# Loads of V on one queue, w_in further up, and a new order for the first quarter of an attention and MLP kernel

## The chip, the cores and the metric

The kernel runs on one core of one Trainium2 chip. The metric is the device time of one execution in microseconds (us). Time before is the median of three runs; one more execution was recorded by the profiler.

## The reference

```python
# q, k, v: (8, 8, 576, 64), batch, heads, tokens, head size; float32
q_d, k_d, v_d = means over groups of 4 tokens          # 144 pooled tokens
out_up    = repeat(softmax(scale * q_d @ k_d.T) @ v_d, 4 times along the tokens)
out_local = softmax(scale * q @ k.T where |i - j| < 4) @ v
attn = out_up + out_local
x = attn.transpose(0, 2, 1, 3).reshape(4608, 512)      # 8 batches x 576 tokens
h = x @ w_in                                           # 512 x 2048
g = h - tanh(h)
out = g @ w_out                                        # 2048 x 512, float32
```

So it is a coarse attention over pooled tokens plus a narrow band attention, for every head, followed by an MLP over the tokens of all batches.

## The kernel before

**Work and its units.** Heads are worked in 32 pairs; pair p belongs to batch p // 4. One pair goes through these steps, with their lines in before (the changed code is one line longer from line 409 on, so that there the same steps read one higher). SyncE loads q, k into staging tiles `st` (L389, for later pairs into `Tw` and other tiles that are free at that time) and V in two halves, one per head, into `vst` (`load_v`, L415). Casts to bf16 give `qr` (L550) and `vw` (L476). TensorE transposes q, k (L557 and L580 for what is left over), copies take them to `kt`, `kq` (L562, L567, L612, L617). TensorE sums groups of four tokens (L664, L667), and a cast puts them into `qkd` (L672); for later pairs sums `half` (L638, L649, L653) and L643 do it on POOL or DVE. Scores: L701 and L711 (band), L717 (pooled). ScalarE (ACT) takes the exps into `E` (L722, L726, L730), the band mask is multiplied in at L757, on DVE or POOL. V is pooled by L507 and copied to `vp` (L511). The 18 matmuls of L771 give the outputs with their sums; r = 1/sum (L787), `ln` = output times r (L789), both on DVE. TensorE transposes back (L814), `od` (L818 on ACT, L820 on DVE) holds the pooled part, and two joins (L807) write the pair's rows of `xT`. From pair 8 on, DMA transposes issued by SyncE take the place of some of the TensorE ones.

**MLP.** One block is 512 tokens of a batch (64 are left over per batch and done apart, L996, L1114 and others). h = L848, 64 matmuls of 128 x 512 for a block that is done plainly (block 0 and 1 are); tanh on ACT (L860); the subtraction into `gT` on DVE (L863). `mm2` for block 0 is L1142, 64 matmuls; later blocks use L1284, with sums `Tw` of parts of w_out that DVE makes once (L1193). w_in comes in four tiles of 512 KB, issued by GpSimd (POOL, `load_w`, L457), and w_out likewise (L461). Block 1's L848 needs all four `xT` parts of pairs 4 to 7.

**What sets the order.** The program records every operation with its reads and writes in a `Plan`; `emit` then issues them in the order of the table `TURNS` (two digits in base 62 per operation). `ENGINES` has one letter per operation that may run on more than one engine (A, D, P for ACT, DVE, POOL), in the order in which they are recorded. `BANKS` seats results in PSUM. `FILL` puts warm-up matmuls ahead of an operation, and `BEHIND` lists pairs of operations of which the second waits for the first, between DVE and POOL. Each engine works through its own instructions in that order, and an instruction that issues a DMA waits in the order of its engine like any other.

Of the kernel before, what the change touches and what calls it, by code (L numbers as in the profile page):

```python
# [101 lines left out]
def kernel(  # L102
# [51 lines left out]
    TURNS = (
        "000I0J0G0H0307060E0F0K0L04050Q0R010O0P0W0X0e0f0C0M0N0S0T100Y0Z110g0h020a0b1215130D0A160U"
        "0V171H1P18141I0B1J191L1Q1A1K1R221M1N0m0n0i0j1O242R231T1j1k1B251S1C1f1d1g1e1u1U0c0d1W1v1w"
        "2S1y0k0l1x2Z091V2I2J0y2T082G2H1z1D2V291E2W0o0p261F2U1X1l1m212X27201n1o2z1Y2b1Z0z391p1q2a"
        "0q0r2d282c2n2o1r1G2e311h1i1s2f2p2q2g2A2K2L322Y1t3A3B2B2O2y5H2C3C3D302D2P3G5I332E1a353E0s"
        "0t2M2N5J34362v2h2F373N3O5K5L5P2i1b5e5f383F0u0v5M5S2w5N2r2s2j5O5Q3H5U5R3I3J5v662Q2k683K5B"
        "5T1c635E5V3L3d2l5C5x2m643j3k5y3M3l3e5D5F3f3g5X3p3q5W0w0x3m3h3v3r3n3w3i3P3Q5w3s5Y3t2t2u3o"  # L160
        "413x615k5l3y3u5z3z4243604744404D4E4548623T3U495Z654A464F4G4B4J6b5a674H4P3V3W4Q6B4R2x4K4L"
        "4I696c4S5g5h4M6e4C4N3X3Y3R3S5s5b6g6A4V4W4b4O6d4c5c4d4T4X5d4Y6U4h5t4U4i4Z5m5n4j4e4k6T4a6C"
        "4l4n6V6D4o6E4f4t4u4p6W4v4g6X6Z6f6F6Y7A6j4z4q6G5G4w4m504r513Z3a526H6a5556534s577B6Q4x5854"
        "7f7C6R7g4y6h3b3c7D597E72887F6i8d8e5A5u7I6k7G71896l7l6m74758E8F7H8j736n6y76778k6z966o7J6K"
        "6L977K6I6J9C7L5i5j7m8K6p5q5r7M6w6x8L7N7r7O5o5p8p78CF6M6N9D79CC7s6u6v7x9f8Q6q6r7y9g6s6t8R"
        "9Z9I9a8S8q9T9b9cCG7z9h9i7X9jCE6O6P7Y7b9k7P7Q7Z9J9l9v9w7c6SCB8v9t9u7d8w9U7V7WCD9O8x9P7R7S"
        "7eAA9m9W7h9V9X9Y7i7a7n9QCH7o7j9nAB7p7k7t70ACAD809d9o9p849eAGAd7uA1A27qAe9q9zA0AH7vA79r81"
        "7T7U9sA8BD857w82ELEMAIAh9x9y86838AAgAJ8B878GAiAjCI8H8C8MAEAM8VAFATAU8I8NAVAW8DAm8WAKAbAc"
        "Ao8J8O8ZB0B18XAL8aBGBH8fAq8PAn8gAN8Y8bBFB2B38l8h8cA9ApAk8m8iBEAt8rAOBMBIBJ8sAP8n8yAr8z8o"
        "8tDt92BcBdBN908u93AXAYBAAl91DyIgIh989EBaBbAs9FBBENEO94CJBOBPBgBh99BQ9K95Dx9AAuBiDzE09G9L"  # L170
        "9BBqEaBKBrBLE39HA5A6CLCMEJEKAv9MBsAwE4B8B9BtBRBkBlByBTEb9NE5A3A4BjE6E7BzEcEdBSCREACSCKAQ"
        "8T8UE8C0E1C1CYARBUC6CZCoE2C7C8CpBVF8BWCuC9CAEgCvEHEIASAxD0EiIcIdAyBXEhEkD2AZAaBYDuD3BZB6"
        "B7AfF7EjAzD8EPEQElEVD9ERESEeDvBmEfIeIfBuE9BvF9FAEmDEBnEBBwFDB4B5DGEnBxDHFfEwExBoDMEXEYEC"
        "IFDNEDCXEWEuEvC2F2C3ETEUDSCaFEC4BpCbBCCgIGC5F3ChFVFWFeFFCmFGFgEEEFCNFICnCTFHCUFTFUDTFBFJ"
# [232 lines left out]
    def load_v(p):  # L407
        b, j, s = p // NP, p % NP, seat_v(p)
        for i in range(2):
            base = v[b, 2 * j + i]  # L410

            aside = (p, i) in ASIDE

            def issue(i=i, base=base, aside=aside):
                (nc.scalar if aside else nc.sync).dma_start(out=vst[s][:, i], in_=bass.AP(  # L415
                    tensor=base.tensor, offset=base.offset,
                    ap=[[D, 128], [STEP * D, NT], [1, D]]))
# [1138 lines left out]
```

## Time and profile before

| what | value |
|---|---|
| median of three runs | 309.12 us (308.51 to 309.83) |
| profiled execution | 309.13 us |
| its span | 307.4 us |
| mean granted TensorE clock | 0.992 |

The span is the time from the first to the last recorded instruction; about 1.7 us of the execution lie outside. PE is TensorE's matmuls, PEld its weight loads, DVE is VectorE, ACT ScalarE, POOL GpSimd, SP SyncE; a name with q behind it (ACTq) is that engine's instruction queue, where DMA issues and waits stand. A releaser, given as `<-`, is what ended an engine's idle time.

### The profile page before, as it was taken

How to read it: one execution, taken by the hardware profiler on the slowest of the kernel's cores; microseconds unless marked ns; L12 is line 12 of the kernel's file. 1: busy time of each engine (PE TensorE's matmuls, PEld its weight loads, DVE VectorE, ACT ScalarE, POOL GpSimd, SP SyncE). 2: the span in 40 equal slices, each digit the busy share in tenths (PEclk: the TensorE clock that was granted, in tenths of full speed). 3: DMA queues.
4: the chain of work that ended last, by engine and by line, in shares of the span. 5: the costliest groups of instructions: out<-in, count | busy, mean ns of one | idle time of the engine just before them, and what ended most of it. 6: DMA issues, size and time to landing. Idle time of an engine off the chain costs nothing.

```text
span 307.4 us, 8109 instructions
## 1 busy us (share of the span) xinstructions
PE 296.4 (96%) x3091; PEld 210.9 (69%) x3100; DVE 266.6 (87%) x493; ACT 224.1 (73%) x403; POOL 157.2 (51%) x213
## 2 busy tenths in 40 slices
PE   8598999999999999999999999999999999999994
PEld 3476555545577755875577755555988888889983
DVE  2578888679998988999998889999999999998783
ACT  2588786279888786988958988898877898875300
POOL 5247756026864466337873278456524364626550
PEclk9979999999999999999999999999999999999999
DMA  7999999999999999999899999979989426000333
GB/s 220 271 264 249 246 228 152 210 235 220 218 241 281 242 216 234 291 175 273 210 262 220 284 222 173 278 193 260 188 227 218 146 28 189 1 3 2 136 122 87
DMA packets 121191, 60.83 MB, mean 198 GB/s; under 512 B 88896, under 2 KB 119104, under 8 KB 121152
## 3 DMA queue, kind: packets, MB, share of 16 engines
q1 hardware_dynamic: 114656, 54.94, 76.5%
q0 software_dynamic: 4224, 4.19, 8.3%
q10 hardware_dynamic: 2272, 1.18, 1.6%
q8 instruction: 24, 0.39, 0.5%
q14 instruction: 15, 0.12, 0.1%
HBM read 44.04 MB, written 9.44 MB: 174 GB/s over the span
## 4 chain that ended last, share of the span: by engine, by line
PE 88%; DVE 5%; DMA 4%; issue 1%; ACT 1%; ACTq 0%; SPq 0%; DVEq 0%
PE ps L1284 27%; PE ps L848 26%; PE ps L958 8%; PE ps L771 6%; PE ps L996 5%; PE ps L1142 4%; PE ps L701 3%; PE ps L1114 2%; PE ps L1081 2%; DMA st<-in_q_dram 2%; DMA sr<-in_q_dram 2%; PE ps L814 1%; DVE E L757 1%; PE ps L717 1%; PE ps L507 1%
## 5 line engine op out<-in xcount | busy, mean ns | idle before, releaser
L848 PE MATMUL ps<-xT,w_in_sb 128*128 128x512 bf16 x384 | 91.5, 379 | 0.0
L1284 PEld LDWEIGHTS <-gT 128*128 128x128 bf16 x672 | 64.5, 98 | 12.3
L863 DVE TENSOR_TENSOR gT<-ps,u 128x512 bf16<-128x512 f32 x96 | 64.2, 684 | 6.8 <-ACT u L860 5.6
L860 ACT ACTIVATE u<-ps 128x512 f32<-128x512 f32 x96 | 56.4, 599 | 16.3 <-PE ps L848 14.5
L848 PEld LDWEIGHTS <-w_in_sb 128*128 128x128 bf16 x384 | 35.4, 98 | 35.6
L550 POOL CAST qr<-st 128x512 bf16<-128x512 f32 x42 | 25.4, 613 | 41.3 <-DVE Tw L1193 15.5
L1284 PE MATMUL ps<-w_out_sb,gT 128*128 128x256 bf16 x336 | 43.4, 273 | 0.0
L1284 PE MATMUL ps<-Tw,gT 128*128 128x256 bf16 x336 | 42.5, 273 | 0.0
L722 ACT ACTIVATE E<-ps 128x912 bf16<-128x912 f32 x32 | 29.9, 934 | 7.1 <-PE ps L711 5.8
L789 DVE TENSOR_TENSOR ln<-ps,r 128x768 bf16<-128x768 f32 x32 | 30.6, 955 | 0.8
L628 ACT COPY kt<-kq 128x576 bf16<-128x576 bf16 x23 | 27.3, 1185 | 1.4 <-DMA kq<-qr 1.1
L757 DVE TENSOR_TENSOR E<-E,mask 128x1152 bf16<-128x1152 bf16 x31 | 23.5, 760 | 3.8 <-ACT E L726 3.5
L771 PEld LDWEIGHTS <-E 128*128 128x128 bf16 x576 | 21.9, 98 | 6.0 <-DVE E L757 1.4
L638 POOL TENSOR_TENSOR half<-kq 128x576 f32<-128x576 bf16 x16 | 20.5, 1279 | 8.4 <-ACT u L860 3.5
L730 ACT ACTIVATE E<-ps 128x576 bf16<-128x576 f32 x32 | 21.0, 657 | 1.4 <-PE ps L717 1.4
L771 PE MATMUL ps<-vw,E 128*128 128x65 bf16 x320 | 19.2, 195 | 1.3 <-DVE E L757 1.0
L643 POOL TENSOR_TENSOR qkd<-half 128x288 bf16<-128x288 f32 x21 | 16.7, 797 | 5.8 <-DVE r L787 2.0
L1219 DVE TENSOR_TENSOR gT<-gT 128x2048 bf16<-128x2048 bf16 x14 | 17.2, 1231 | 0.2
L1370 POOL TENSOR_TENSOR y<-y,keep 128x512 f32<-128x512 f32 x8 | 10.2, 1278 | 13.4 <-DVE E L757 4.8
L996 PE MATMUL ps<-xT,w_in_sb 128*128 128x128 bf16 x256 | 16.8, 219 | 0.0
L1306 ACT COPY y<-ps 128x512 f32<-128x512 f32 x19 | 11.0, 587 | 7.5 <-PE ps L1284 6.7
L771 PE MATMUL ps<-vpr,E 128*128 128x65 bf16 x128 | 16.5, 195 | 0.0
(183 smaller groups left out, 596.4 us busy)
## 6 DMA issues: line engine op xcount, KB each, us to landing
vst<-in_v_dram SPq DMA_DIRECT2D x54, 160.0 KB, 4.2
st<-in_q_dram SPq DMA_DIRECT2D x28, 256.0 KB, 3.7
st<-in_k_dram SPq DMA_DIRECT2D x28, 256.0 KB, 5.0
out_dram<-y SPq DMA_DIRECT2D x14, 512.0 KB, 4.3
v<-in_v_dram SPq DMA_DIRECT2D x20, 256.0 KB, 2.7
w_in_sb<-in_moe_w_in_dram POOLq DMA_DIRECT2D x4, 512.0 KB, 8.4
w_out_sb<-in_moe_w_out_dram POOLq DMA_DIRECT2D x4, 512.0 KB, 6.6
vr<-in_v_dram SPq DMA_DIRECT2D x8, 128.0 KB
```

Of the source, the lines that this page charges most:

```text
L550: (eng, ns, lambda dst=dst, src=src, fn=fn: fn(out=dst, in_=src), port)
L628: ("ACT", 1180, lambda: A.copy(out=ktv, in_=src), False),
L722: A.activation(out=E[s][:, :, E0:E0 + 456], in_=at(s1)[:, :, PS0:512], func=AF.Exp, scale=SCALE)
L757: eng.tensor_tensor(out=el, in0=el, in1=mask.unsqueeze(1).to_broadcast([128, 2, S]), op=ALU.mult)
L771: T.matmul(po[:, hh, 65 * n:65 * n + 65], E[s][:, hh, e:e + 128], vv, start=start, stop=stop)
L789: op("DVE", 960, lambda: V.tensor_tensor(out=ln[s].rearrange("p n (h d) -> p h n d", d=D), in0=blocks()[:, :, :, 0:64], in1=r[s].unsqueeze ...
L848: T.matmul(at(name)[:, 0, :], w_in_sb[:, dc, fc * 128:(fc + 1) * 128], xT[dc][:, c0:c0 + S].rearrange("p (c g) -> p c g", c=4)[:, :, 0:128 ...
L860: op("ACT", 600, lambda: A.activation(out=u[us], in_=at(name)[:, 0, :], func=AF.Tanh), reads=[("hd", kb, fc)], writes=[("u", us)], uses=[n ...
L863: op("DVE", 690, lambda: V.tensor_tensor(out=gT[g][:, fc, :], in0=at(name)[:, 0, :], in1=u[us], op=ALU.subtract), reads=[("hd", kb, fc), ( ...
L958: T.matmul(at(("hz", kb, G, bk))[:, 0, 256 * x:256 * x + 256], left(k, x), right(k), start=(first and x == 0 and k == 0), stop=(k == 1), s ...
L996: T.matmul(at(name)[:, 0, 128 * f:128 * f + 128], w_in_sb[:, dc, (f0 + f) * 128:(f0 + f) * 128 + 128], xT[dc].rearrange("p (b c g) -> p b ...
L1284: T.matmul(dst, left[:, f, 128 * j:128 * j + 128], right[:, f, :], start=(first and e == 0 and f == 0 and (j == 0 or apart)), stop=(e == 1 ...
```

## The change

Three things. First, `ASIDE` is replaced by an empty `WAY`: before, the first halves of V for pairs 2 and 3 were issued by ScalarE, now SyncE issues all of them. Second, the tables: the first 719 of the 2263 entries of `TURNS` are put in another order (this reaches to about 90 us), and the rest is the same entry for entry. The set of operations is the same. Third, `ENGINES` moves 58 operations to another engine, and `BANKS`, one entry of `FILL` (another bank) and `BEHIND` go with the new order. Of `TURNS` a line stands here for all.

```diff
-        "000I0J0G0H0307060E0F0K0L04050Q0R010O0P0W0X0e0f0C0M0N0S0T100Y0Z110g0h02
...
+        "0I0J0G0H0E0F0K0L0Q0R0O0P0W0X0e0f000307060405010M0N0S0T0Y0Z0g0h0a0b0U0V
...
     ENGINES = (
-        "APADDADAADPPDDPPDDADDDDAPPDADDAADDDPDDDDDAADDADAADDDAAADDDPPAPPPAADAPPPDAAPAPADADPPPDDAA"
-        "APADAAPPPDAAPPDDAAPPPDDAAAADDPDADDAADDDDAPPPDDPPDAAAPPAAPPDDAAPPPAAPPDDPPADDADDADAAPPDAP"
+        "DDADDADDDPPDDAPADDADADDADADDADAADAADDDAADADDADAPAAADDAADDPPPDPPAADADPPPDAAAPAAADDPPDDDDA"
+        "PDAADAPDPDAAPPPDAAPDDPDAAADPPPDADPAAPDDDDPPPDDPPDAAAPPDADPDDAAPPPAAPPDDPPADDADDADAAPPDAP"
...
         "ADPDDPPPDDD"
     )
     BANKS = (
-        "0123453012067016731120212706021330112130022310312010302101013121001113020110023303011200"
-        "2131010210231012301102321001203101010110123031002311201210012130120131010102030210302321"
+        "0123721011626324512321305410230320200313520012100322130311102113011012230320101300011230"
+        "1132100233101032011002301001203101010110123031002311201210012130120131010102030210302321"
     )
     FILL = (
-        "15717 2b71 2A71 3B41 2D11 5S31 3H31 6671"
+        "15717 2b71 2A71 3B41 2D11 5S31 3H01 6671"
     )
     BEHIND = (
-        "0211 1H12 1D1V 0z20 1t2f 5I30 5Q5N 635B 5w5W 6562 6c2x 6d6A 5u6i AACD ABCH AmAF AnAL DxC"
-        "J F8CZ FfFD DFFn MUFt GAGb IrJ6 JNK7 MZJs NBKu OELA LqNn ODLO O7OQ QoNy RYOp RZP8 T3Rd S"
-        "WPQ PiSi TVTU TaRk TPUO TnUY TmTO WZU7 WeWc WfVu XWX6 XcXP Z5Yy ZqZ4 ZpZH"
+        "0211 1H12 1B19 2y2f 5v5W 5C6A 6b6c 7A6Z 717C 7273 7H6i 9fCG 9aCH 9TCI AACF AnAF A9AL BEA"
+        "k DxCJ F8CZ FfFD DFFn MUFt GAGb IrJ6 JNK7 MZJs NBKu OELA LqNn ODLO O7OQ QoNy RYOp RZP8 T"
+        "3Rd SWPQ PiSi TVTU TaRk TPUO TnUY TmTO WZU7 WeWc WfVu XWX6 XcXP Z5Yy ZqZ4 ZpZH"
     )
 
     const = ctx.enter_context(tc.tile_pool(name="const", bufs=1))
...
     def seat_qk(p):
         return p if p < 2 * NP else p % NST
 
-    ASIDE = ((2, 0), (3, 0))
+    WAY = {}
 
     def seat_v(p):
         return p if p < 9 else (p - 9) % NVST
...
         for i in range(2):
             base = v[b, 2 * j + i]
 
-            aside = (p, i) in ASIDE
-
-            def issue(i=i, base=base, aside=aside):
-                (nc.scalar if aside else nc.sync).dma_start(out=vst[s][:, i], in_=bass.AP(
-                    tensor=base.tensor, offset=base.offset,
-                    ap=[[D, 128], [STEP * D, NT], [1, D]]))
-            load(680 if aside else 500, issue, [("vst", s, i)], 940, 10 * p - 3000 + 5,
-                 eng="ACT" if aside else "SP")
+            eng = WAY.get((p, i), "SP")
+
+            def issue(i=i, base=base, eng=eng):
+                {"SP": nc.sync, "ACT": A, "POOL": GP}[eng].dma_start(
+                    out=vst[s][:, i], in_=bass.AP(
+                        tensor=base.tensor, offset=base.offset,
+                        ap=[[D, 128], [STEP * D, NT], [1, D]]))
+            load({"SP": 500, "ACT": 680, "POOL": 770}[eng], issue, [("vst", s, i)], 940,
+                 10 * p - 3000 + 5, eng=eng)
 
     def load_v4(p):
         b, h0, s = p // NP, 2 * (p % NP), p % NV4
```

What it does to the order of three engines, at the places that matter below. On ACT, near the program's start, before: `vst3` and `vst2` are the V tiles of pairs 3 and 2, `E0` and `E1` the exps of even and odd pairs, `qkd1` the pooled q and k of pair 1.

```order
L617 COPY kq0_94<-rT0_81 128x4x16
L612 COPY kt1_97<-rT0_81 128x4x16
L415 DMA vst3_86<-in_v_dram 128x5x64
L415 DMA vst2_85<-in_v_dram 128x5x64
L672 CAST qkd1_100<-ps_138 128x2x144
L722 ACTIVATE E0_113<-ps_138 128x2x456
L726 ACTIVATE E0_113<-ps_138 128x2x120
L730 ACTIVATE E0_113<-ps_138 128x2x2x144
```

The same place after:

```order
L551 CAST qr1_93<-st1_74 128x2x4x64
L673 CAST qkd0_99<-ps_138 128x2x144
L551 CAST qr0_92<-st2_75 128x2x4x64
L613 COPY kt1_97<-rT0_81 128x4x16
L727 ACTIVATE E0_113<-ps_138 128x2x120
L731 ACTIVATE E0_113<-ps_138 128x2x2x144
L723 ACTIVATE E0_113<-ps_138 128x2x456
L673 CAST qkd1_100<-ps_138 128x2x144
L723 ACTIVATE E1_114<-ps_138 128x2x456
```

The two DMA issues are gone; `qkd` of pair 0, a cast of pair 1 and one of pair 2 stand ahead of the exps, the exps of pair 0 are in another order, and `qkd1` follows them instead of preceding them.

On POOL, where its first casts and loads of weights stand, before (`w_in_sb` is w_in, `vrs` and `vrp` are sums over the left-over tokens of V):

```order
L550 CAST qr1_93<-st1_74 128x2x4x64 x2
L442 TENSOR_TENSOR vrp_107<-vrs_106 128x64
L550 CAST qr0_92<-st2_75 128x2x4x64
L445 TENSOR_TENSOR vpr0_111<-vrp_107,hsel_108 128x520
L476 CAST vw1_89<-vst1_84 128x10x64
L457 DMA w_in_sb_71<-in_moe_w_in_dram 128x4x512
L476 CAST vw3_91<-vst3_86 128x10x64
L550 CAST qr1_93<-Tw1_135 128x2x4x64 x2
L457 DMA w_in_sb_71<-in_moe_w_in_dram 128x4x512
```

And after:

```order
L551 CAST qr1_93<-st1_74 128x2x4x64
L439 TENSOR_TENSOR vrs_106<-vr0_104 128x128
L443 TENSOR_TENSOR vrp_107<-vrs_106 128x64
L458 DMA w_in_sb_71<-in_moe_w_in_dram 128x4x512
L541 CAST rr1_80<-sr1_78 128x2x4x64
L458 DMA w_in_sb_71<-in_moe_w_in_dram 128x4x512 x2
L650 TENSOR_TENSOR half_98<-kt0_96 128x144x2
L551 CAST qr1_93<-Tw1_135 128x2x4x64
```

The first tile of w_in is issued behind one cast and two sums, where before casts of q, k and V for three pairs stood ahead of it; the second and the third are issued together; the casts of `vw` are on other engines at this place.

On DVE, ahead of block 1: the outputs of pairs 6 and 7 (`ln0`, `ln1`), the joins into `xT2`, `xT3` and the sums `Tw`, before:

```order
L757 TENSOR_TENSOR E1_114<-E1_114,mask_66 128x2x576
L550 CAST qr0_92<-st0_73 128x2x4x64
L787 RECIPROCAL r1_116<-ps_138 128x12
L789 TENSOR_TENSOR ln1_118<-ps_138,r1_116 128x2x6x64
L807 TENSOR_TENSOR xT2_69<-ps_138,od0_121 128x3x4x28
L807 TENSOR_TENSOR xT2_69<-ps_138,od0_121 128x2x4x30
L820 COPY od1_122<-ps_138 128x144
L807 TENSOR_TENSOR xT3_70<-ps_138,od1_122 128x3x4x28
L807 TENSOR_TENSOR xT3_70<-ps_138,od1_122 128x2x4x30
L1193 TENSOR_TENSOR Tw2_136<-w_out_sb_72 128x1024
L1193 TENSOR_TENSOR Tw0_134<-w_out_sb_72 128x1024
```

And after:

```order
L790 TENSOR_TENSOR ln0_117<-ps_138,r0_115 128x2x6x64
L1194 TENSOR_TENSOR Tw0_134<-w_out_sb_72 128x1024 x2
L1194 TENSOR_TENSOR Tw2_136<-w_out_sb_72 128x1024
L788 RECIPROCAL r1_116<-ps_138 128x12
L790 TENSOR_TENSOR ln1_118<-ps_138,r1_116 128x2x6x64
L1194 TENSOR_TENSOR Tw1_135<-w_out_sb_72,Tw0_134 128x1024
L821 COPY od1_122<-ps_138 128x144
L808 TENSOR_TENSOR xT3_70<-ps_138,od1_122 128x3x4x28
L808 TENSOR_TENSOR xT3_70<-ps_138,od1_122 128x2x4x30
L644 TENSOR_TENSOR qkd0_99<-half_98 128x2x144
L808 TENSOR_TENSOR xT2_69<-ps_138,od0_121 128x3x4x28
L808 TENSOR_TENSOR xT2_69<-ps_138,od0_121 128x2x4x30
```

Three sums of w_out now stand (two and one) between `ln` of pair 6 and `r` of pair 7 and a fourth ahead of the joins, the joins of pair 6 come last, and the mask of pair 7 (`E1`) is no longer on DVE; POOL has it.

More of the change, by code (lines that the diff above doesn't have):

```diff
@@ L154 @@
     TURNS = (
[L155 to L169, printed above, removed]
@@ L170 @@
-        "8tDt92BcBdBN908u93AXAYBAAl91DyIgIh989EBaBbAs9FBBENEO94CJBOBPBgBh99BQ9K95Dx9AAuBiDzE09G9L"
-        "9BBqEaBKBrBLE39HA5A6CLCMEJEKAv9MBsAwE4B8B9BtBRBkBlByBTEb9NE5A3A4BjE6E7BzEcEdBSCREACSCKAQ"
+        "0I0J0G0H0E0F0K0L0Q0R0O0P0W0X0e0f000307060405010M0N0S0T0Y0Z0g0h0a0b0U0V0C1011021215130D0A"
+        "16171H1P1814080c1j0i1J0k1f1I1Q1d1A1g190B1u1l1m1K0j0m0o2I2G1n0l1R1e1k1N1B1S1U1L221C1M1W1p"
+        "2H1O1T2n1h23242o1D262R1w25270p2p2q1x2T2S2V1v1V0y290n0d0z201y2Z1z212U6q2K2M1E0q2W2Y392z3A"
@@ new lines @@
+        "2a1r1F1s3N282X1X2b2d1Y1Z6s1G2A0r2c2e3B2B2C2J2g3P1a7T2O2P2f1b1c2r2h2i1q302t5e5k3D31352j36"
+        "2y3334322D2E383C0s3G2k09375S1o2F3d1t2v3E3F3e3j2w3H5U2l2m0u5P3k3p3v5I5H3w5Q3I3J3q3r0t5R3K"
+        "3x5J3L5L3M5K5N3f3g5M5O2N3h3i3s3l3t3y3u3m3n3o0w3z4066685T2u5V4142630v434445474864652Q5X4D"
+        "49465W4A4B4C1i4E4F5v6t3V3W67694J4K4L4G4M5B4H4I4N5E5F6A4P4Q3R3S4R4O4S6B4T4V4W5x5y3O4X4Y4b"
+        "4c5g5h3T4d4U4Z4a4e4f4h5C5D4i4j614g5Y5Z5l9x4k0x3X5w5z604l4n4o4t4z4u4v504w6T3Z3a2L2x5a4p4q"
@@ new lines @@
+        "4m624x4r4y3Y516e6g4s5s5t52535556575b5c3Q6C6U6c546V587f5988895m7P6D5d6b6d3b3c6E8d8e5A6W6Z"
+        "6X6F6G6Y6a6H7A6f6j96979C7U2s5G7B6Q6h6R8j8k7g7l7D7C7E7F5f7m71745n7372766K6I3U7I5i7G9D5j8E"
+        "8F6O776i6k6l6m9I7r9JAX6J7H5u9z8KCBCC6y755q6w9v6u6zCG6n8p8q7J9w8v5r789f6x8L8Q7V8R7K6v7L8w"
+        "7M9O9PCD797N7O7s7x7y6P9h9g6o6p9i9ZCH8x8S9Q5o6M5p7X7z7Y9t9u7b6L9a9jCE9k9b6N7Z9lCI7a9T9U9m"
+        "9V7h7i7j7c7n7o6r7k7d7e7t7u6S9W8084CF9X7p7qAAA17W9c9n9oAB9Y9p9d7R7v7w7Q8182AG9e8A70858B8C"
@@ L172 @@
+        "83Ad9q9r9sA7Ag8G8HA8868D87ACAe8I8JAHAIAJAK7SAhAM8M8V8W8N8O8Z8aBDADAEAmAF8P8f8gAoATAnApAL"
+        "AV8b8XAiAj8YA9Ak8l8mAq8c8r8s8h8i8n8oAN8y8z9293AOAP8t8uBA989E9FB2AbB0BGBaArAYAt90AlBBA0BE"
+        "ENA2BFBIAcBMBNBHEO949yDtAsIg91CJBOBcBdBPBgBhELEM99AWBQ9K95B3AUDx9AAuBiDyDzE09G9L9BBqBJB1"
+        "EaBKBrBLE39HA5A6CLCMEJEKAvIhBb9MBsAwE4B8B9BtBRBkBlByBTEb9NE5A3A4BjE6E7BzEcEdBSCREACSCKAQ"
         "8T8UE8C0E1C1CYARBUC6CZCoE2C7C8CpBVF8BWCuC9CAEgCvEHEIASAxD0EiIcIdAyBXEhEkD2AZAaBYDuD3BZB6"
```

## The prediction

> **What bounds the kernel now.** Line numbers are those of before. I read the page first (busy times, the slices, the TensorE clock):
>
> ```profile
> PE 296.4 (96%) x3091; PEld 210.9 (69%) x3100; DVE 266.6 (87%) x493; ACT 224.1 (73%) x403; POOL 157.2 (51%) x213
> ...
> PE   8598999999999999999999999999999999999994
> ...
> PEclk9979999999999999999999999999999999999999
> ```
>
> TensorE is busy 96% of the 307.4 us span. Its only weak slices are the second, the last, and the third with a lowered clock. So a reordering can gain only what TensorE loses at the start, and can lose wherever it lets TensorE run dry. Next I read the busy times by stretch. Columns: the stretch, its length, busy time of PE, PEld, DVE, ACT, POOL, the granted clock, the DMA share, GB/s:
>
> ```profile
> 8.00:15.00 7.00, 4.02 (x69) 3.02 (x67) 4.18 (x15) 3.18 (x9) 2.04 (x4) 1.00 1.18 270
> 15.00:30.00 15.00, 12.89 (x215) 10.29 (x216) 11.92 (x30) 13.40 (x29) 8.60 (x12) 0.89 1.19 256
> 30.00:49.00 19.00, 19.00 (x175) 10.52 (x174) 16.59 (x38) 14.08 (x30) 12.67 (x18) 1.00 1.12 217
> 49.00:64.00 15.00, 14.84 (x135) 7.92 (x135) 11.92 (x25) 6.14 (x14) 2.79 (x4) 1.00 0.96 193
> 64.00:90.00 26.00, 25.89 (x270) 15.61 (x269) 23.01 (x39) 23.50 (x42) 16.21 (x22) 1.00 1.08 243
> 90.00:200.00 110.00, 109.89 (x1092) 73.56 (x1092) 99.45 (x168) 90.01 (x154) 61.85 (x87) 1.00 1.04 238
> ```
>
> TensorE stands 2.98 us in 8–15 and 2.11 us in 15–30, then 0.0 to 0.2 us per stretch. ACT is nearly full in 15–30 (13.40 of 15). In 64–90 three engines are close to full at once. From the DMA share and the GB/s: the loads run without a gap in 8–30. What ACT does in the weak stretch is in its timeline (start, duration, what ended the idle time):
>
> ```profile
> 8.99 0.34 ACT L612 COPY kt<-rT 128x64 bf16<-128x64 bf16 x1
> 11.17 1.95 ACTq L415 DMA_DIRECT2D vst<-in_v_dram  x2
> 13.15 0.40 ACT L672 CAST qkd<-ps 128x288 bf16<-128x288 f32 x1 [3.82 <-DMA st<-in_q_dram]
> 13.45 0.94 ACT L722 ACTIVATE E<-ps 128x912 bf16<-128x912 f32 x1
> ...
> 14.52 0.67 ACT L730 ACTIVATE E<-ps 128x576 bf16<-128x576 f32 x1
> ```
>
> ACT does nothing from 9.33 to 13.15 us. Its queue stands at the two issues of V halves, for pairs 3 and 2; the second is only through at 13.11, and the copy qkd and all exps of the first pair are queued behind. TensorE then waits for that copy (the waits of PE: sum, times, longest):
>
> ```profile
> PE ps L717 <- ACT qkd L672: 2.3, 1, 2.3
> ```
>
> The chain of waits goes over the same place (start, length):
>
> ```profile
> 6.86 5.86 DMA st<-in_q_dram
> ...
> 17.86 1.16 PE ps L771 x18
> ...
> 25.61 0.55 PE ps L771 x18
> ...
> 28.83 0.97 DVE ln L789
> ...
> 31.47 2.59 PE ps L848 x12
> ```
>
> From the stall, attention of the first four pairs (its outputs are the L771 groups) leads to ln of the fourth pair and so to the first matmuls L848 of the MLP. From there on TensorE is never short for long.
>
> **The change part by part.** *V halves from ACT to SP.* ACT's stall, 3.82 us, goes. On ACT the change also puts casts qr of pairs 1 and 2 and qkd of pair 0 ahead of the exps, and the exps of pair 0 no longer stand behind qkd of pair 1. Those are two casts at about 0.5 (this cast took 0.43 on DVE, row below) and one at 0.40, 1.3 us, done within the old gap. From 9.33 that gives 10.7; the exps (13.45 to 15.19, 1.74 us) end near 12.4 instead of 15.19. So the head of the chain comes 2.8 us earlier by the sum of ACT's work, and at most 3.8 earlier.
>
> SP now issues two more transfers. They cost SP's queue and not a byte:
>
> ```profile
> 6.44 0.88 SPq L389 DMA_DIRECT2D st<-in_q_dram  x2
> ...
> 11.95 1.94 SPq L415 DMA_DIRECT2D vst<-in_v_dram  x2
> ```
>
> That is 0.97 us per V half where the queue is full, 1.9 us for both. Behind them stand the loads for pairs 4 to 7, which attention needs after 30 us: zero. The loads of q for pairs 2 and 3 stay ahead of them (issued from 6.44); the tenth load lands here, where DVE casts it:
>
> ```profile
> 12.84 0.43 DVE L550 CAST qr<-st 128x512 bf16<-128x512 f32 x1 [0.40 <-DMA st<-in_q_dram]
> ```
>
> Nothing of the change brings that load forward, so pair 1's pooled part still can't begin before 12.8. The gain is one pair's head start, not a shorter chain per pair.
>
> The Trainium skill ("Trainium Kernel Development and Optimization", Key Constraints) says that transfers issued from SP, ACT and POOL share the same 16 DMA engines, so that issuing from several engines saves only issue time. By that, taking two issues off ACT would give back two issue times, under 1 us. The trace differs: the idle time before the next ACT instruction is 3.82 us, since the issue waits in ACT's instruction order; I go by the trace.
>
> *w_in further up.* The rows of the four tiles, and what the page has of their landing beside an SP load (KB each, median us):
>
> ```profile
> L457 POOL DMA_DIRECT2D w_in_sb<-in_moe_w_in_dram x4: 748/794/944, 19.4 to 33.6; - x4
> ```
>
> ```profile
> st<-in_q_dram SPq DMA_DIRECT2D x28, 256.0 KB, 3.7
> ...
> w_in_sb<-in_moe_w_in_dram POOLq DMA_DIRECT2D x4, 512.0 KB, 8.4
> ```
>
> The first tile moves from 19.4 to about 10.7 us: in the order of POOL only one cast and two small sums stand ahead of it now, instead of casts and V casts of pairs 1 and on. No wait of the trace is for w_in, so landing earlier gains nothing. It can cost: 512 KB (0.524 MB) taken from the SP loads, at the 264 GB/s of a full DMA (between 270 and 256), is 2.0 us at most; zero if it finds gaps, of which there are none. Over its 8.4 us it moves 62 GB/s, a quarter of the total. The total was 270 with a second queue beside SP's (the V halves), and 256 over 15–30. I take 1.4 us, nearer the upper end: the total hardly grows. V halves and q, k of the next pairs come later by that.
>
> *Front, summed.* The stall 3.8 less 1.4 for the tile: 2.4 us earlier at the joins of block 0 and at the first L848. Upper end 3.8 (no cost). Lower end 0.5: 3.82 less 2.0 for the tile and 1.3 for the work moved onto ACT, if nothing covers it. ACT's own work allows it: 3.18 + 13.40 = 16.6 of the 22 us in 8–30.
>
> *The boundary to block 1.* Here the change gives something back. Rows of PE, DVE and POOL:
>
> ```profile
> 48.91 0.38 PE L848 MATMUL ps<-xT,w_in_sb 128*128 128x512 bf16 x1
> ...
> 58.35 0.50 PE L814 MATMUL ps<-ident,ln 128*128 128x128 bf16 x6
> 58.68 4.91 PE L1142 MATMUL ps<-w_out_sb,gT 128*128 128x512 bf16 x21
> 63.52 0.38 PE L701 MATMUL ps<-kq,kt 64*128 64x112 bf16 x8
> ...
> 64.02 1.47 PE L848 MATMUL ps<-xT,w_in_sb 128*128 128x512 bf16 x6
> ```
>
> ```profile
> L757 DVE TENSOR_TENSOR E<-E,mask x31: 740/751/906, 14.7 to 251.6; 128x1152 bf16<-128x1152 bf16 x31
> L757 POOL TENSOR_TENSOR E<-E,mask x1: 2374/2374/2374, 153.2 to 153.2; 128x1152 bf16<-128x1152 bf16 x1
> ```
>
> ```profile
> L1193 DVE TENSOR_TENSOR Tw<-w_out_sb x4: 681/684/685, 59.6 to 65.8; 128x1024 bf16<-128x1024 bf16 x4
> ```
>
> ```profile
> 56.82 0.23 DVE L787 RECIPROCAL r<-ps 128x12 f32<-128x12 f32 x1 [1.90 <-PE ps L771]
> 57.09 0.96 DVE L789 TENSOR_TENSOR ln<-ps,r 128x768 bf16<-128x768 f32 x1
> ...
> 58.88 0.23 DVE L820 COPY od<-ps 128x144 bf16<-128x144 bf16 x1 [0.41 <-PE ps L814]
> 59.15 0.52 DVE L807 TENSOR_TENSOR xT<-ps,od 128x336 bf16<-128x336 bf16 x2
> ...
> 61.57 0.46 DVE L643 TENSOR_TENSOR qkd<-half 128x288 bf16<-128x288 f32 x1
> ```
>
> Before, 30 matmuls L1142 stood between the output L771 of pair 7 and block 1's first L848, and 10 more behind it. At 0.22 us each (22 of them from 58.68 to 63.52) that was 6.6 us of cover; the joins x ended at 59.67, and L848 came at 64.02, no wait. After, all of L1142 is done before block 1 begins, and only 20 stand behind the output of pair 7: with the back transposes L814 (0.5) and the scores of pair 8 (0.5, from 63.52 to 64.02) that is 5.4 us of cover. Under it lies: r 0.23, ln 0.96, transposes with their two hand-offs 0.83 (ln's end at 58.05 to od's start at 58.88), a T sum 0.68, od 0.23, joins 0.52, qkd 0.46, joins 0.52, and a hand-off at either end, about 0.2 each by the same rows: 4.8. In front stand three T sums, 3 × 0.68 = 2.05, which DVE now has ahead of r of pair 7. They run while the mask of pair 7 is on POOL (2.37 instead of 0.75). If they fit wholly under it, nothing is lost (4.8 against 5.4). If not at all, it is 4.8 + 2.05 − 5.4 = 1.5 late. I take the middle, 0.8, since POOL's longer mask hides at most 1.6 of the 2.05. The 10 matmuls moved ahead lengthen one side and shorten the other by the same 2.2 us: zero. From 90 us on the order is as before: zero.
>
> *Other edits.* One warm-up filler sits in another PSUM bank, some DVE to POOL waits go or come, PSUM seats change: work of the same first stretch, inside the 0.5 to 3.8.
>
> *Sum.* −2.4 + 0.8 = −1.6 against the profiled 309.13 (span 307.4 and 1.7 around it), which is the median of the runs (309.12) to 0.01: **307.5 us**. A measurement here can tell about 0.5%, 1.5 us, from no change.
>
> **The rivals.** *A, the forecast, part kept:* 306.5 to 308.2.
>
> *D, all of it kept.* The tile costs the front nothing: 3.8 − 0.8 = 3.0, 306.1. For it: POOL was busy 2.04 of 7 us and DVE 4.18. Against: the DMA share is at its top in both stretches.
>
> *B, w_in takes equal turns with the SP loads.* Then a tile lands in 2 × 0.524 MB / 264 GB/s = 4.0 us and holds the SP loads back by the full 2.0 us; with the second and third tile issued together near 22 us, pair 3's data come later again by the 1.4 that one cost in the sum; 3.8 − 2.0 − 1.4 = 0.4 is left, with the boundary at nothing: 308.7. Against it: 8.4 us to landing. The Trainium skill ("DMA: Bandwidth & Descriptors", SWDGE vs HWDGE vs iDMA) says that each DMA engine has 16 queues and takes them in turn, with the software-issued transfers in queues of their own. By that a tile gets a half; the trace's quarter speaks against it, unless SP fills more than one queue.
>
> *C, slower: block 1 starts dry.* Place: the first L848 of block 1. If the mask on POOL begins late (behind other work of POOL), pair 7's output is 2.37 − 0.75 = 1.6 later, and the T sums then still stand before it or are done. Both uncovered: 1.6 + 1.5 = 3.1 us in place of the 0.8 in the sum, and TensorE catches none of it up. It decides when pair 7's masked E comes over 0.5 us after TensorE has run through the matmuls in front of it: those behind it cover only 5.4. Then 309.1 − 2.4 + 3.1 = 309.8 at the front gain that I take, and 311.7 at its lower end of 0.5. What makes pair 7 late would have kept the front back too, so the small gain goes with this case: 311.0. For it: no L1142 is left for TensorE, and in 64–90 DVE and ACT have 3 us and less to make it up. Against: DVE is busy 11.92 of 15 in 49–64 and can wait.
>
> *E, the change only moves the wait:* TensorE waits for the tenth load (12.84) in any order, and pair 1 comes no earlier; 309.1.
>
> **How the numbers follow.** A 0.48, of which 0.36 lies under 307.6 and 0.12 above; D 0.10; B 0.11; C 0.28, of which 0.23 lies above 310.7; E 0.03. Faster by over 0.5%: 0.36 + 0.10 = 0.46. Within: 0.12 + 0.11 + 0.05 + 0.03 = 0.31. Slower: 0.23. Low end 305.8, just under D (0.05 lie below it); high end 311.2, inside C (0.10 above). A's own range is 306.5 to 308.2.
>
> **What would show it.** Right: in the changed kernel ACT has no idle time over 1 us between 9 and 13; exps of pair 0 end near 12.4; the chain's L771 groups and the first L848 stand 2 to 3 us earlier; w_in's first tile is issued near 10.7. Boundary: TensorE stands under 1 us at block 1's first L848. Wrong: over 1.5 us of TensorE idle there with a join L807 as releaser (C); SP's loads of pairs 1 and 2 landing 2 us or more later (B); the lead at the first L848 under 1 us; or new standing times of TensorE after 90 us, where I count none.

## The result, and the profile after

The changed kernel takes 313.28 us (median of four runs, 312.48 to 316.26) against 309.48 us of the kernel before on the same chip: a ratio of 1.0153, 95% interval 1.0122 to 1.0184. It is 3.8 us or 1.5% slower, where 307.5 us was predicted. Its profiled execution took 312.48 us, with a span of 310.8 us. Some executions of a kernel are some per cent longer at a lower clock; the medians below are of all executions of a run, the ratios leave those out. Line numbers below are those of the changed kernel (one higher than before's) unless before or a kernel built on it is named.

The page: busy times, TensorE's slices, its clock.

```profile
PE 297.9 (96%) x3093; PEld 210.4 (68%) x3100; DVE 269.4 (87%) x497; ACT 225.7 (73%) x403; POOL 154.8 (50%) x209
...
PE   8878799999999999999999999999999999999995
...
PEclk9999999999999999999999999999999999999999
```

The clock is full throughout in this execution, so its loss is not a matter of clock. Before had lost some clock behind ACT's stall. Its stretch 15–20, and the same one after:

```profile
15.00:20.00 5.00, 4.42 (x60) 3.71 (x59) 3.29 (x10) 4.21 (x10) 2.33 (x3) 0.66 1.20 272
```

```profile
15.00:20.00 5.00, 4.84 (x95) 3.93 (x94) 4.33 (x11) 3.36 (x9) 0.00 (x0) 1.00 1.19 241
```

The weak slice moved: before it was the second (5), now the third to fifth are weak (7, 8, 7). The stretches, columns as in the prediction, with 30 to 49 cut in two:

```profile
8.00:15.00 7.00, 6.13 (x98) 4.91 (x96) 5.65 (x19) 6.69 (x15) 1.95 (x4) 1.00 1.17 239
15.00:30.00 15.00, 11.51 (x189) 8.28 (x188) 11.38 (x29) 10.35 (x24) 5.59 (x8) 1.00 1.20 250
30.00:35.00 5.00, 3.26 (x24) 1.58 (x23) 3.72 (x10) 2.88 (x6) 1.34 (x2) 1.00 1.20 223
35.00:49.00 14.00, 13.97 (x128) 7.43 (x128) 11.61 (x23) 11.78 (x23) 5.22 (x8) 1.00 1.07 233
49.00:64.00 15.00, 14.74 (x148) 8.44 (x148) 10.18 (x22) 7.16 (x15) 8.39 (x9) 1.00 1.05 212
64.00:90.00 26.00, 25.77 (x262) 15.11 (x261) 24.65 (x48) 20.98 (x38) 13.45 (x20) 1.00 0.88 214
```

In 8–15 TensorE is idle for 0.87 us, where it was 2.98: the gain is there, 2.1 us. In 15–30 it is idle for 3.49 (before 2.11), and in 30–35 for 1.74 (before none). By 35 us the gain is given back and more: both kernels have then done 16 of the matmuls L848 (L849), but the changed one has done 72 of the output matmuls L771 (L772) where before had done 90, and 40 of the score matmuls L701 (L702) where before had done 48.

ACT's timeline in the first stretch shows the step that was aimed at:

```profile
9.79 0.41 ACT L673 CAST qkd<-ps 128x288 bf16<-128x288 f32 x1
...
11.07 0.67 ACT L731 ACTIVATE E<-ps 128x576 bf16<-128x576 f32 x1
11.60 0.96 ACT L723 ACTIVATE E<-ps 128x912 bf16<-128x912 f32 x1
```

ACT no longer stands, and the exps of pair 0 end at 12.56 instead of 15.19. The chain of waits shows what comes next (start, length):

```profile
12.73 7.72 DMA vst<-in_v_dram
...
22.37 0.74 PE ps L772 x18
...
26.32 0.93 DVE vw L477
27.26 1.27 DVE E L758
28.58 0.76 PE ps L772 x18
...
33.09 1.90 DVE gT L864 x3
35.03 0.38 PE ps L1525
```

The long piece is a half of V for pair 2, issued by SyncE at 12.73 and landed at 20.45. Pair 2's outputs (22.37) are still 3.1 us earlier than before (25.45 in TensorE's timeline), but pair 3's, behind a cast of its own V at 26.32, begin 0.9 us later than before, at 28.58 instead of 27.72 (the fourth group L771 of before). The first matmul of the MLP is much earlier all the same. Before:

```profile
30.87 0.38 PE L848 MATMUL ps<-xT,w_in_sb 128*128 128x512 bf16 x1
```

After:

```profile
26.64 0.39 PE L849 MATMUL ps<-xT,w_in_sb 128*128 128x512 bf16 x1
```

The new order only puts it ahead of other work, as the counts at 35 us show. The last piece of the chain is new. TensorE's timeline and its longest waits:

```profile
31.66 1.62 PE L849 MATMUL ps<-xT,w_in_sb 128*128 128x512 bf16 x6
35.03 0.38 PE L1525 MATMUL ps<-lT 128*128 128x512 bf16 x1 [1.74 <-DVE gT L864]
```

```profile
PE ps L1525 <- DVE gT L864: 1.7, 1, 1.7
PE ps L508 <- ACT vw L477: 1.5, 2, 1.3
```

L1525 is a warm-up matmul of `FILL`, whose result nobody uses. The entry `6671` puts it into PSUM bank 7 ahead of the scores of pair 5; the change left this entry as it was. But in the new `BANKS` bank 7 holds a result h of the MLP, and the filler waits until DVE has read it for `gT`. The scores behind it were not held by anything else that the chain shows: their k and q were ready at 32.46, and with the filler in another bank (an experiment below) TensorE runs through this place.

SyncE's queue reaches q of pair 8, the first load of block 2, much later. Its row before, and its row after:

```profile
36.69 1.11 SPq L389 DMA_DIRECT2D st<-in_q_dram  x1
```

```profile
45.33 0.69 SPq L389 DMA_DIRECT2D st<-in_q_dram  x1
...
57.24 0.43 DVE L551 CAST qr<-st 128x512 bf16<-128x512 f32 x1 [2.00 <-DMA st<-in_q_dram]
```

DVE now waits 2 us for that load, and the mask of pair 6, which TensorE's outputs need, stands behind the cast. In this kernel TensorE has matmuls L1143 to do meanwhile: it is idle for 0.26 us in 49–64.

The delay that stands at 35 us is still there at block 1, and it grows behind it. Block 1 begins here, without a wait:

```profile
65.24 2.32 PE L1143 MATMUL ps<-w_out_sb,gT 128*128 128x512 bf16 x10
67.49 0.38 PE L702 MATMUL ps<-kq,kt 64*128 64x112 bf16 x8
...
67.98 4.28 PE L849 MATMUL ps<-xT,w_in_sb 128*128 128x512 bf16 x19
```

That is 3.96 us later than before (64.02), of which 2.16 are the ten matmuls of `mm2` now done ahead of it: 1.8 us late. At 255 us the same instruction of DVE (L982, L981 before) stands at 257.34 instead of 254.73, 2.6 late; the span ends 3.4 late. The last step, from 2.6 to 3.4, is at one place:

```profile
261.89 0.53 DVE L808 TENSOR_TENSOR xT<-lT 128x336 bf16<-128x336 bf16 x2 [1.03 <-DMA lT<-ln]
```

DVE waits there for a DMA transpose, 3.18 us after its issue ended (258.71). Before, the same join began 2.06 us after it (256.10 to 258.16), and without a wait. TensorE behind it waits for 0.6 us (L959).

### The profile page after: what moved, and what is told of

The parts are those of the page before. It is cut to its first block, busy times and chain, and to the rows that moved or that the text cites. A ratio compares the mean times of both kernels' runs of the same rounds, so it can differ in the third digit from the quotient of the medians.

```text
span 310.8 us, 8106 instructions
## 1 busy us (share of the span) xinstructions
PE 297.9 (96%) x3093; PEld 210.4 (68%) x3100; DVE 269.4 (87%) x497; ACT 225.7 (73%) x403; POOL 154.8 (50%) x209
## 4 chain that ended last, share of the span: by engine, by line
PE 67%; DMA 9%; DVE 8%; SPq 5%; issue 5%; POOL 4%; ACT 1%; ACTq 0%; POOLq 0%; DVEq 0%
PE ps L849 24%; PE ps L1285 21%; PE ps L997 4%; PE ps L772 4%; PE ps L959 3%; DMA vst<-in_v_dram 2%; SPq L415 2%; PE ps L702 2%; PE ps L1115 2%; DMA v<-in_v_dram 2%; PE ps L1143 2%; DMA sr<-in_q_dram 2%; PE ps L1082 1%; DMA lT<-ln 1%; DMA S<-in_v_dram 1%
## 5 line engine op out<-in xcount | busy, mean ns | idle before, releaser
L849 PE MATMUL ps<-xT,w_in_sb 128*128 128x512 bf16 x384 | 91.8, 380 | 0.0
L849 PEld LDWEIGHTS <-w_in_sb 128*128 128x128 bf16 x384 | 35.5, 98 | 35.9 <-issue 0.5
L772 PEld LDWEIGHTS <-E 128*128 128x128 bf16 x576 | 21.4, 97 | 5.9 <-DVE E L758 2.4
L772 PE MATMUL ps<-vw,E 128*128 128x65 bf16 x320 | 19.0, 193 | 1.1 <-DVE E L758 0.9
L644 POOL TENSOR_TENSOR qkd<-half 128x288 bf16<-128x288 f32 x19 | 15.3, 803 | 5.4 <-DVE kt L630 2.6
L477 ACT CAST vw<-vst 128x640 bf16<-128x640 f32 x22 | 15.7, 729 | 1.9 <-DMA vst<-in_v_dram 1.8
```

The source lines that it names most:

```text
L772: T.matmul(po[:, hh, 65 * n:65 * n + 65], E[s][:, hh, e:e + 128], vv, start=start, stop=stop)
L849: T.matmul(at(name)[:, 0, :], w_in_sb[:, dc, fc * 128:(fc + 1) * 128], xT[dc][:, c0:c0 + S].rearrange("p (c g) -> p c g", c=4)[:, :, 0:128 ...
```

## The experiments

All ratios are to the kernel before, run on the same chip (its medians 308.8 to 309.5 us). "After" as a base means the changed kernel.

**The parts alone, on the kernel before.** *V on SyncE, order as before:*

```diff
-    ASIDE = ((2, 0), (3, 0))
+    ASIDE = ()
```

> The kernel before with the one part alone: the two V halves issued by SyncE, at the places that they had in the order (there ahead of q, k of pair 4), no other edit. T1 in its form (place in SP's queue decides, ACT's issue was a real stall): ACT's 3.8 us gap at 9.3 to 13.2 shrinks to under 1.5, exps of pair 0 end 1.5 to 2.5 us earlier, time 0.5 to 2 us below before (307.5 to 309). If the gap was only a place where a later wait shows (next wait: q, k of pairs 2, 3 and DVE), the time is the same as before to 0.5 us.

308.71 us, ratio 0.9979 (0.9964 to 0.9994): faster, by 0.65 us and no more. Its exps of pair 0 end at 12.35, so ACT's stall is gone as forecast. The head of its chain of waits, and TensorE's waits:

```profile
7.72 6.21 DMA vst<-in_v_dram
14.01 0.74 ACT vw L476
14.79 0.46 PE ps L507 x5
```

```profile
PE ps L507 <- ACT vw L476: 1.1, 1, 1.1
PE ps L507 <- POOL vw L476: 0.9, 1, 0.9
```

A landing V half has taken the place of ACT's issue: it was issued at 7.72 and landed at 13.93, and 2.0 us of new waits stand in pooling V (L507). The clock in 15–20 is 1.00 here too.

*w_in's first tile up, alone* (its entry 0q, in before's order):

```diff
-1S1C1f1d1g
+1S1C0q1f1d1g
```

> The kernel before with the other part alone: the first w_in tile issued behind the sums of V's left-over (about 11.6 us instead of 19.4). If the tile takes bandwidth from SP's loads one for one (0.52 MB at 0.25 MB per us): the V halves and q, k behind it land 2 us later, pair outputs 1 and 2 come 0.5 to 2 us later, time 0.5 to 2 us above before. If it finds room (the value taken in the prediction, 1.4 us of delay, mostly hidden): the same to 0.5 us.

310.32 us, 1.0041 (1.0022 to 1.0059), 1.3 us slower, the prediction's price of the tile (1.4).

*Five loads up, alone.* The change also reorders loads of SyncE that its name does not speak of: q and k of pair 10, a V half of pair 10 and the left-over tokens of V of batch 2 now stand ahead of q of pair 8, k of pair 11 right behind it; 1.1 MB in all. In before they come later. Their entries, put up into before's order:

```diff
-2f2p2q2g
+2f2p2q6q6r2g
...
-3O5K
+3O6s6t5K
...
-3Q5w
+3Q7T7U5w
...
-4i4Z5m
+4i4Z9x9y7P7Q5m
```

> The kernel before with the one thing alone that the run of the five loads took back from the changed kernel: those loads for batch 2 (q, k of pair 10, k of pair 11, a V half of pair 10, left-over V; 1.1 MB) ahead of the load of q of pair 8 on SyncE, everything else as before. T3 (they take their time from loads needed sooner): q of pair 8 is issued 3 to 9 us later than the 36.7 us of before; slower than before by 0.5 to 2.5 us (309.6 to 311.6) if DVE, which casts it at 54.5, has to wait; the same to 0.2% if the load still lands ahead of that cast, and then the five loads cost only together with the later start that the changed kernel's SyncE already has there.

308.98 us, 1.0004 (0.9991 to 1.0016): nothing. Its q of pair 8 is issued at 41.18 instead of 36.69, lands at 51.18, and that is still ahead of its cast at 54.9.

So the named parts, alone on the old order, add up to +0.2%, and the pulled loads to nothing. The rest of the 1.5% belongs to the new order, or to the parts together with it.

**Taken out of the changed kernel, one at a time.** *Fillers into free banks:*

```diff
-        "15717 2b71 2A71 3B41 2D11 5S31 3H01 6671"
+        "15717 2b71 2A71 3B41 2D41 5S31 3H01 6621"
```

> The changed kernel with two warm-up fillers in the bank that their own operation opens anyway (bank 2 instead of 7 ahead of the scores of pair 5, bank 4 instead of 1 ahead of the back transposes of pair 1); nothing else. Theory T2 (the fillers kept their old bank numbers while the new seating gives these banks to MLP results, so TensorE stands for a subtraction that it doesn't need): the 2.3 us of standing at 33 to 35 us shrink to under 0.8, and the time falls by 1.0 to 2.0 us against the changed kernel, to 311.3 to 312.3. Theory T1 (V of pairs 2 and 3 lands late, and everything after is a consequence): TensorE only stands a little later, for banks that the same subtractions free; under 0.5 us gained.

315.35 us, 1.0198 (1.0164 to 1.0232): not faster than after, rather slower, though the intervals overlap. The stall itself is gone (TensorE is busy 5.00 of 5 us in 30–35), but q of pair 8 holds everything:

```profile
30.00:35.00 5.00, 5.00 (x43) 2.21 (x42) 4.36 (x11) 4.84 (x11) 1.35 (x2) 1.00 1.20 216
...
49.00:64.00 15.00, 10.54 (x80) 5.20 (x78) 5.71 (x13) 4.06 (x8) 5.03 (x5) 0.81 0.83 179
```

```profile
51.59 0.89 SPq L389 DMA_DIRECT2D st<-in_q_dram  x1
...
58.70 0.43 DVE L551 CAST qr<-st 128x512 bf16<-128x512 f32 x1 [6.66 <-DMA st<-in_q_dram]
...
59.85 0.46 PE L772 MATMUL ps<-vw,E 128*128 128x65 bf16 x5 [4.46 <-DVE E L758]
```

With the front earlier, POOL issues the second tile of w_out at 40.24 (after: 43.40) and the others likewise; SyncE's loads beside them take 10 us and more to land, and q of pair 8 goes out at 51.59, 6 us later than in after. DVE is ready 3 us earlier and waits 6.66 us, TensorE 4.5 us, and the granted clock in 49–64 is 0.81. That the tiles of w_out are what slows these loads is read from the rows; no run moved them.

*w_in's first tile late* (after, with the tile held behind r of pair 0; issued at 17.4):

```diff
-2K2M1E0q2W2Y
+2K2M1E2W2Y
...
-1Y1Z6s1G
+1Y1Z0q6s1G
...
-Z5Yy ZqZ4 ZpZH"
+Z5Yy ZqZ4 ZpZH 0q1Y"
```

> The changed kernel with the first w_in tile held back until r of pair 0 is done (about 17.3 us, issue at 11.5 before). T1: the second V half of pair 2 lands at 18.0 to 18.8 instead of 20.45, ACT's 1.8 us of standing at its V cast go, the outputs of pairs 2 and 3 (L772) come 1.3 to 2.0 us earlier, and the time falls by 1.0 to 1.8 us, to 311.5 to 312.3. T2 alone: pair outputs move, but TensorE still stands 2 us at the filler; under 0.7 us gained. If the tile took only a quarter of the bandwidth at no cost to the others, the V half lands at 20 as before.

315.77 us, 1.0211 (1.0176 to 1.0245). The outputs of pairs 2 and 3 come 2.2 and 2.0 us earlier than in after (they begin at 20.19 against 22.37 and at 26.58 against 28.58), so the tile did hold V back; and again the gain runs into q of pair 8 (cast at 59.43):

```profile
PE ps L772 <- DVE E L758: 4.5, 3, 4.0
```

*The five loads back behind q of pair 8* (after, the reverse of the edit above), and *this together with the fillers:*

```diff
-"...5m7P6D..."
+"...5m6q6r6s6t7T7U9x9y7P7Q6D..."
```

> The changed kernel with five loads for batch 2 (q, k of pair 10, k of pair 11, a V half of pair 10, the left-over of V) moved on SyncE from ahead of the load of q of pair 8 to right behind it, where the kernel before has them or later; 1.1 MB. New theory T3: the table also pulls these loads up, so q and k of pairs 7 and 8 land late, and DVE stands for the q of pair 8 (2.0 us in the changed kernel, 6.7 us once the front was faster) with the mask of pair 6 queued behind it. T3 expects: DVE's wait for that load under 0.5 us, time 0.8 to 2 us below the changed kernel (311.3 to 312.5). Rival (the front alone sets the time, T1 with T2): TensorE had matmuls L1143 to cover that wait, so under 0.4 us changes.

> The same loads moved back and the two fillers in their own banks. T2 with T3 (each was hidden by the other): 2 to 3.5 us below the changed kernel, 309.8 to 311.3, and 4 us or more below the kernel with the fillers alone; TensorE's standing at 33 to 35 us and at the output of pair 6 both under 0.8 us. If T3 is false: as with the fillers alone, 315.

312.14 us, 1.0123 (1.0086 to 1.0161), and 311.28 us, 1.0089 (1.0055 to 1.0123). Here the fillers gain: from the one to the other 0.9 us, half of their stall, though the intervals overlap. In the second the cast still waits 1.3 us for q of pair 8, and a new wait shows, for a V half of pair 8, which SyncE now issues at 65.98:

```profile
64.00:90.00 26.00, 23.96 (x268) 14.81 (x269) 23.67 (x41) 21.75 (x39) 14.90 (x22) 1.00 0.85 207
...
PE ps L508 <- ACT vw L477: 2.9, 2, 1.8
```

*That, with both V halves of pair 8 put right behind the DMA transposes:*

```diff
-8F6O776i
+8F5q5r5o5p6O776i
```

> The changed kernel with the fillers in their own banks, the five loads of batch 2 behind q of pair 8 (both as in an earlier run), and now the two V halves of pair 8 at the head of the loads that follow the transposes of pair 8, as in the kernel before, instead of the second one behind nine others. Theory T3 in its wide form (the table's new order of SyncE's loads is what costs: each load is needed at a set time, and TensorE stands where one comes late): ACT's 2.1 us for that V half at 68 to 70 us and TensorE's 1.8 us behind it go; 1 to 2 us below the run without this edit, 309.3 to 310.3, level with before. Rival (the boundary of block 1 has a limit of its own, DVE at 24 of 26 us): under 0.5 us changes.

310.77 us over 12 runs, 1.0041 (1.0023 to 1.0058). Fillers and order of loads together are 1.1 of the 1.5%.

*The tile of w_in late on top of these*, once behind r of pair 0 without the V of pair 8, once behind the mask of pair 0 with it (in both its entry 0q of `TURNS` moves along):

```diff
-Z5Yy ZqZ4 ZpZH"
+Z5Yy ZqZ4 ZpZH 0q1Y"
```

> As the one before, and the first w_in tile held back until r of pair 0. T1 on top of T2 and T3: another 0.5 to 1.5 us down, 308.8 to 310.5, since the V halves of pairs 2 and 3 land 2 us sooner. If V's landing was not what held the front: no more than 0.3 us away from the one before.

```diff
-Z5Yy ZqZ4 ZpZH"
+Z5Yy ZqZ4 ZpZH 0q1V"
```

> The changed kernel with three edits of earlier runs (fillers in their own banks; five loads of batch 2 behind q of pair 8; V of pair 8 at the head of its loads), which together stand 0.4% above before, and the first w_in tile held back until the mask of pair 0 is through (about 14.7 us instead of 11.5). The tile alone cost the kernel before 0.4%. If the early tile is the rest of the loss: 0.3 to 0.5% down, level with before (309 to 309.6), V of pair 2 lands 1 us or more sooner. If the rest has another place (the late DMA transpose at 260 us, 1 us): no change to 0.2%. If the tile now comes too late for the MLP's first matmuls: TensorE waits for w_in at 24 to 27 us and the time is higher.

313.63 us, 1.0129 (1.0086 to 1.0173), and 311.09 us over 12 runs, 1.0066 (1.0042 to 1.0090). The first is too late, TensorE waits for the tile:

```profile
PE ps L849 <- DMA w_in_sb<-in_moe_w_in_dram: 2.8, 1, 2.8
```

The second (tile issued at 15.0) has the earliest first L849 of all: 24.52, after 26.64, before 30.87. It keeps nothing of it. Its chain and TensorE's longest wait:

```profile
43.06 12.78 DMA st<-in_q_dram
...
55.86 0.43 DVE qr L551
56.29 0.68 DVE E L758
...
PE ps L772 <- DVE E L758: 3.7, 3, 3.2
```

**V earlier.** *The first halves of pairs 2 and 3 back on ACT, in the new order* (their entries of `TURNS` stand behind the copy to kt of pair 1):

```diff
-    WAY = {}
+    WAY = {(2, 0): "ACT", (3, 0): "ACT"}
```

> The changed kernel with the two V halves issued by ACT again, at the place that they have in ACT's order before (behind the copy to kt of pair 1), nothing else. T1: V of pairs 2 and 3 lands 1 us or more sooner, but ACT stands 1.5 to 3 us ahead of the exps of pair 0 again; the two about cancel, 0 to 1.5 us slower than the changed kernel (313.3 to 314.8). If the V part were what costs the change its time: 1 us or more faster.

315.69 us, 1.0219 (1.0189 to 1.0248). ACT's stall returns, and the granted clock falls to 0.50 in 15–20:

```profile
PE ps L702 <- ACT E L731: 4.3, 1, 4.3
```

*V of pairs 2 and 3 ahead of q, k of pair 4* (on top of the kernel with 1.0041), and *the same idea on before* (V on SyncE, one V half to the head of the loads):

```diff
-16171H1P1814080c1j0i1J0k1f
+16171H1P1814080c0i0j0k0l0m0n0o0p1j1J1f
```

> As the one before, and the four V halves of pairs 2 and 3 issued by SyncE right behind those of pairs 0 and 1, ahead of q, k of pair 4. T1: second V half of pair 2 lands 1 us sooner (19.4), that of pair 3 2 to 3 us sooner (about 21), ACT's 1.8 us at the V cast shrink by 1; another 0.5 to 1.5 us, 308 to 309.5. If q, k of pair 4 (now later) hold the front instead: no change or up to 1 us slower.

```diff
-"0V171H1P
+"0V0c0d171H1P
...
-    ASIDE = ((2, 0), (3, 0))
+    ASIDE = ()
```

> The kernel before with its two V halves on SyncE, and the second V half of pair 1 ahead of those of pairs 2 and 3 and of q, k of pair 4. With the halves on SyncE alone, the cast of V of pair 1 stood till 18.4 us for this half. T3 in its wide form (order of the loads by when they are needed): that cast starts 2 to 4 us earlier, the output of pair 1 1 us or more earlier, 0.3 to 1.2 us below the kernel with the halves alone; 307.5 to 308.4. If pair 1 is not what holds the front: the same as the halves alone, 308.7.

314.54 us, 1.0163 (1.0135 to 1.0191), and 313.19 us (309.26 to 316.17), 1.0082 (1.0044 to 1.0119). In the first the load that was overtaken becomes the wait:

```profile
ACT qr L551 <- DMA Tw<-in_k_dram: 5.5, 1, 5.5
PE ps L772 <- ACT vp L512: 5.3, 1, 5.3
```

In the one execution of the second that was profiled it is q of pair 4 (DVE waits 5.8 us for it, TensorE 5.5 for the cast). But that execution took 314.32 us, above all that the ratio counts (309.26 to 313.25), so where these lose their time isn't shown.

**The join at 261 us.** Four more DVE instructions at the start (DVE has 493 in before, 497 in after), to see whether their number alone moves that join:

```diff
-    op("DVE", 70, lambda: V.memset(vrp[:, D:D + 1], 4.0), writes=["vrp"])
+    def five():
+        for _ in range(5):
+            V.memset(vrp[:, D:D + 1], 4.0)
+    op("DVE", 70, five, writes=["vrp"])
```

> The kernel before with four more memsets of 64 elements on VectorE at about 6.5 us, where it is idle; the changed kernel has four VectorE instructions more than before. All runs of the changed order so far show 3.2 us from the issue of the last DMA transpose to the join that reads it (at 260 us), all runs of the old order at most 2.1, and TensorE loses about 1 us there. If the place of the instructions in VectorE's stream (their number ahead) makes this: 3.2 us here too and 0.5 to 1 us slower than before. If not: 2.1 us and the same time to 0.2%.

309.16 us, 0.9997 (0.9982 to 1.0011), and the join begins 2.06 us after the issue, as in before. That is not it. In the traces of kernels on the new order this gap is 3.1 to 3.4 us, each time with a wait of DVE of 1.0 to 1.3 us, in those on the old order 2.06 or 2.07 and without one; why is open.

## Why the prediction was wrong, point by point

**Right: ACT's stall.** It is gone, and the exps of pair 0 end at 12.56 (forecast 12.4). The first L849 comes 4.2 us earlier (forecast 2 to 3), but this sign was met without the gain that it stood for, since the new order moved it. The tile of w_in is issued at 11.5 (forecast 10.7), and alone it costs 1.3 us (forecast 1.4).

**Wrong: "Behind them stand the loads for pairs 4 to 7, which attention needs after 30 us: zero".** This is the main failed step: it put SyncE's queue behind the V halves at nothing. It has two faults. First, the other halves of V for pairs 2 and 3 stand in the same queue, and they are needed before 30 us: pair 2's landed at 20.45 and pair 3's at 23.49, TensorE waited 1.6 us there for casts of V (L508), and pair 3's outputs came 0.9 us late, where 2.4 early was forecast. Second, zero was read from when a load is needed, without the loads behind it. Issues of 2 to 5 us in SyncE's rows (4.71 us at 27.48 the longest) show that an issue can stand there, though not for what, and the DMA share in 35–49 and 49–64 is still 1.07 and 1.05. A load put further up there delays those behind it until one is late. On the old order q of pair 8 went out at 36.69, and even with the five loads pulled up it landed 3.7 us ahead of its cast; on the new one it goes out at 45.33, and what the edits gained for the front was lost at it. The prediction priced w_in's tile against this queue, but did not follow the queue to its end, nor see the five loads pulled up in it. Taking these and the V of pair 8 back, with the fillers, brought 1.0153 to 1.0041; on the old order the five loads cost nothing (1.0004), and the V of pair 8 was not tried there. The two V halves that gave the change its name are not the fault in themselves: alone they gained 0.65 us, and back on ACT in the new order they made it slower (1.0219).

**Wrong in size: the stall's worth, 3.8 us (2.4 with the tile taken off).** Alone, V on SyncE is worth 0.65 us, since there a load of V lands late behind the stall and TensorE waits 2.0 us for its casts. The prediction weighed the Trainium skill ("Trainium Kernel Development and Optimization", Key Constraints), by which issuing from several engines saves only issue time, and set it aside because the trace showed 3.82 us of idle time. By that rule the gain, as the prediction estimated it, would have been under 1 us, and 0.65 was measured. That the size agrees doesn't show the rule's reason: the exps of pair 0 did end 2.8 us earlier (12.35 against 15.19). The trace's wait was real, but what it hid set the time.

**Wrong: "Other edits … inside the 0.5 to 3.8".** The filler in bank 7 stands 1.74 us by itself, and the sum had no term for it. Moved with the filler in bank 1, once the five loads were back, it gave 0.9 us. The entry stands unchanged in both lines of the diff; what changed is whose bank it is.

**Rivals.** A, D and E ask for a time no longer than before's. C named the wrong place and cause: block 1 begins without a wait in the changed kernel, the 0.8 of the sum is zero, and the joins are not late (their last ends at 67.03, L849 begins at 67.98). The stretch ahead of block 1 did go dry in three kernels (4.5, 4.0 and 3.2 us at pair 6's outputs), but from a load, not from POOL's mask or the sums of w_out. B is nearest: loads that hold the rest back. The tile's price in time is the sum's (1.3 against 1.4), while the outputs of pairs 2 and 3 came 2.2 and 2.0 us earlier without it, B's full 2.0. On the Trainium skill's rule of turns between queues ("DMA: Bandwidth & Descriptors", SWDGE vs HWDGE vs iDMA) no run decides. The row of w_in's four tiles in the changed kernel:

```profile
L458 POOL DMA_DIRECT2D w_in_sb<-in_moe_w_in_dram x4: 746/765/942, 11.5 to 27.9; - x4
...
DMA to landing us min/median/max: 7.7/9.8/11.8
```

At 250 GB/s (15–30 us) a tile alone on all engines would take 0.524 MB / 250 GB/s = 2.1 us, so it had about a fifth to a quarter of them; but SyncE's loads beside it are of several sizes, and no run held their number fixed.

**"Nothing after 90 us".** About 0.8 us arises at 261 us, at the DMA transpose (2.6 to 3.4 late). Another 0.8 arises between 64 and 97 us (1.8 to 2.6 late), where DVE is busy 24.65 of the 26 us of 64–90; no experiment took that apart.

**What stays open.** Of the 1.53%, 1.1 are accounted for by the filler, the five loads and the V of pair 8, and single steps among them (0.30, 0.34 and 0.48%) lie at the edge of what their intervals tell apart. The last 0.4% is as much as w_in's tile costs alone, but taking the tile back (1.0066) did not give it back, so that is not its cause, or the wait for q of pair 8 hides it. The two late losses, 1.6 us together, would be enough for it too; the one at 261 us is in every trace of a kernel on the new order.

The best kernel of all is the smallest change: V's halves on SyncE with the old order, 0.9979 of before, and faster than either kernel.

## What to carry to other kernels

When a load queue is full, each load in it has a latest time; price a reordering by listing every load that the new order moves, with its landing against its first reader, to the point where the queue runs empty. A wait that ends in an issue is worth only what the data behind it lets through, so look at when that data lands before counting the wait as gain. When a table that assigns buffers changes, read again the entries of other tables that name these buffers, even if they stand unchanged.
